# Hash attention and serf feed-forward on one core: a new erf polynomial, log1p and abs re-split over the engines, units taken in pairs

## Chip, cores, metric

One core of a Trainium2 chip, everything in float32. The metric is device time in microseconds (us); each kernel was timed in several executions beside the kernel before on the same chip. Engines: PE is TensorE, DVE is VectorE, ACT is ScalarE, POOL is GpSimd. In a profile row such as `L409 ACT COPY h<-h_ps`, L409 is the line of the kernel's source, and `h<-h_ps` says what is written from what.

## The reference

Attention with a hash mask over 4 x 8 heads of 768 tokens and 64 features, then, on x of 3072 x 512:

```python
h = x @ w_in                                            # 512 -> 2048
sp = np.maximum(h, 0.0) + np.log1p(np.exp(-np.abs(h)))  # softplus
g = h * erf(sp)
return (g @ w_out).astype(np.float32)                   # 2048 -> 512
```

The change touches only this second half.

## The kernel before

The feed-forward works in 48 units; a unit is 256 tokens x 512 features, a tile of 128 x 1024. Per unit: 32 matmul instructions into PSUM (`hidden`), elementwise work on ACT, DVE and POOL, and later 16 matmul instructions with w_out (`project`). Cut to what matters:

```python
def exponential(u):
    nc.scalar.activation(out=a, in_=ps, func=AF.Abs)
    nc.scalar.activation(out=a, in_=a, func=AF.Exp, scale=-1.0)
    nc.scalar.copy(out=h, in_=ps)
    nc.gpsimd.tensor_scalar(out=up, in0=a, scalar1=1.0, scalar2=None, op0=ALU.add)
    nc.vector.scalar_tensor_tensor(out=a, in0=up, scalar=-1.0, in1=a, op0=ALU.add, op1=ALU.subtract)

def softplus(u):
    nc.scalar.activation(out=s, in_=s, func=AF.Ln)                    # s is up
    nc.vector.scalar_tensor_tensor(out=s, in0=h, scalar=0.0, in1=s, op0=ALU.max, op1=ALU.add)
    nc.vector.scalar_tensor_tensor(out=s, in0=s, scalar=S_MAX, in1=a, op0=ALU.min, op1=ALU.subtract)
    nc.scalar.activation(out=z, in_=s, func=AF.Square)
    for k in range(len(ERF_P) - 2, -1, -1):                           # six steps
        nc.vector.scalar_tensor_tensor(out=p, in0=prev, scalar=ERF_P[k] / lead,
                                       in1=z if k else s, op0=ALU.add, op1=ALU.mult)

def gate(u):
    nc.scalar.activation(out=d["p"], in_=d["p"], func=AF.Tanh, scale=ERF_P[-1])
    nc.gpsimd.tensor_tensor(out=d["h"], in0=d["h"], in1=d["p"], op=ALU.mult)

# LAG = NG + 2 = 6 units
for n in range(len(units) + LAG):
    if 0 <= n - 2 < len(units): gate(n - 2)
    if n < len(units): hidden(n); exponential(n)
    if 0 <= n - 1 < len(units): softplus(n - 1)
    if n >= LAG: project(...)
```

One thing about the source matters for all that follows: the framework (`tile.TileContext`) puts the instructions into the engines' queues by a schedule of its own.

## Time and profile before

| | before |
|---|---|
| time, median (range) of 7 runs | 1547.7 us (1547.2 to 1549.3) |
| attention ends, feed-forward's products run on | at 784.3 us |
| period of the units (copies of h, 790.8 to 1496.6, over 47) | 15.0 us |
| PE's own work for a unit | 13.8 us |
| from the last copy of h to the end | 48.8 us |
| activation-table loads | 95 |

The table is read from below upwards: PE needs 13.8 us a unit but is served one only every 15.0 us. The lines behind it are in the prediction.

### The profile page before, as it was taken

What the parts mean: (1) busy time and instruction counts of PE and PEld (TensorE: products, weight loads), DVE (VectorE), ACT (ScalarE), POOL (GpSimd) and SP (SyncE); (2) the same over time, 40 slices, a digit from 0 to 9 for tenths busy, and PEclk for the clock granted to TensorE, in tenths of its full rate; (3) what the DMA queues carried; (4) which work ended last, traced back from release to release, by engine and by line L of the source; (5) the groups of instructions that cost most, each with busy time, mean ns of one, the idle gap of its engine ahead of it and who ended that gap; (6) DMA issues with size and microseconds to landing.
All of it is one profiled execution on the core that took longest, in us unless ns stands there. A gap on an engine that the chain in (4) does not pass through costs nothing. (4 is left out here: it accounts for less than half of the span.)

```text
span 1545.4 us, 14597 instructions
## 1 busy us (share of the span) xinstructions
PE 1441.5 (93%) x5248; PEld 808.8 (52%) x5248; DVE 1187.5 (77%) x1865; ACT 758.9 (49%) x1151; POOL 425.2 (28%) x198
## 2 busy tenths in 40 slices
PE   7999999999999999999997898999999999999977
PEld 3444444444445444445575565656565556656543
DVE  6788878888786666666637799888887887878783
ACT  2344444444444444444555554565555555555551
POOL 3333223332220000000013433433433333333340
PEclk9999999999999999999998999999999999999989
DMA  5222222222211011010000000000000000000000
GB/s 157 76 63 67 68 77 76 69 67 63 67 36 42 26 36 41 26 37 6 1 1 0 0 9 13 7 8 7 14 7 7 14 7 7 7 14 8 7 8 27
DMA packets 40704, 49.19 MB, mean 32 GB/s; under 512 B 27308, under 2 KB 27320, under 8 KB 40632
## 3 DMA queue, kind: packets, MB, share of 16 engines
q1 hardware_dynamic: 35856, 31.47, 7.0%
q0 software_dynamic: 4608, 16.78, 3.4%
q8 instruction: 42, 0.69, 0.2%
q14 instruction: 30, 0.25, 0.1%
q10 hardware_dynamic: 168, 0.01, 0.0%
HBM read 41.96 MB, written 6.29 MB: 31 GB/s over the span
## 5 line engine op out<-in xcount | busy, mean ns | idle before, releaser
L392 PE MATMUL h_ps<-xT,w_in_sb 128*128 128x256 f32 x1536 | 353.6, 390 | 50.3 <-ACT h L409 50.0
L457 PE MATMUL o_ps<-w_out_sb,h 128*128 128x512 f32 x768 | 343.7, 601 | 20.7 <-POOL h L446 11.5
L392 PEld LDWEIGHTS h_ps<-xT,w_in_sb 128*128 128x128 f32 x1536 | 296.7, 195 | 122.6 <-ACT h L409 77.4
L325 ACT COPY eT<-tr_ps 128x384 f32<-128x384 f32 x384 | 171.0, 481 | 320.8 <-PE tr_ps L318 319.5
L410 POOL TENSOR_SCALAR up<-a 128x1024 f32<-128x1024 f32 x48 | 161.2, 3358 | 604.1 <-ACT a L408 601.7
L275 PE MATMUL sc<-ka,qa 128*128 128x384 f32 x768 | 299.3, 498 | 11.5 <-ACT e L290 10.9
L432 DVE SCALAR_TENSOR_TENSOR p<-p,a 128x1024 f32<-128x1024 f32 x192 | 266.9, 1392 | 5.2
L333 PE MATMUL av<-eT,vt 128*64 128x384 f32 x768 | 262.1, 491 | 0.0
L457 PEld LDWEIGHTS o_ps<-w_out_sb,h 128*128 128x128 f32 x768 | 147.8, 193 | 191.9 <-issue 175.2
L283 DVE TENSOR_REDUCE m<-sc 128x1 f32<-128x768 f32 x192 | 183.1, 954 | 64.1 <-PE sc L275 60.9
L290 ACT ACTIVATE e<-sc,nm 128x768 f32<-128x768 f32 x192 | 173.9, 906 | 90.1 <-DVE nm L285 87.6
L318 PEld LDWEIGHTS tr_ps<-ident,e 128*128 128x128 f32 x1152 | 126.5, 141 | 120.0 <-issue 50.0
L318 PE MATMUL tr_ps<-ident,e 128*128 128x128 f32 x1152 | 177.2, 281 | 6.9 <-DVE e L303 2.4
L333 PEld LDWEIGHTS av<-eT,vt 128*64 128x64 f32 x768 | 100.0, 137 | 154.1 <-issue 146.0
L446 POOL TENSOR_TENSOR h<-h,p 128x1024 f32<-128x1024 f32 x48 | 119.7, 2494 | 194.3 <-issue 160.2
L275 PEld LDWEIGHTS sc<-ka,qa 128*128 128x128 f32 x768 | 126.5, 192 | 69.5 <-ACT e L290 25.6
L303 DVE TENSOR_SCALAR e<-e,r 128x768 f32<-128x768 f32 x192 | 124.3, 647 | 2.8
L445 ACT ACTIVATE p<-p 128x1024 f32<-128x1024 f32 x48 | 50.7, 1056 | 133.7 <-DVE p L432 133.5
L432 DVE SCALAR_TENSOR_TENSOR p<-a 128x1024 f32<-128x1024 f32 x48 | 74.6, 1554 | 43.1 <-ACT a L427 43.1
L340 DVE COPY xT<-av 64x384 f32<-64x384 f32 x64 | 35.3, 551 | 94.2 <-PE av L333 94.1
L411 DVE SCALAR_TENSOR_TENSOR a<-up,a 128x1024 f32<-128x1024 f32 x48 | 71.4, 1488 | 43.0 <-POOL up L410 43.0
L172 POOL TENSOR_SCALAR keep<-keep 128x512 int32<-128x512 int32 x32 | 73.2, 2286 | 92.8 <-DVE nm L285 56.8
(41 smaller groups left out, 1092.7 us busy)
## 6 DMA issues: line engine op xcount, KB each, us to landing
qa<-in_qkT_dram SPq DMA_DIRECT2D x32, 384.0 KB, 3.5
raw<-in_w_in_dram POOLq DMA_DIRECT2D x16, 512.0 KB, 4.3
raw<-in_w_out_dram POOLq DMA_DIRECT2D x16, 512.0 KB, 3.8
ka<-in_qkT_dram SPq DMA_DIRECT2D x32, 192.0 KB, 3.8
vt<-in_v_dram SPq DMA_DIRECT2D x32, 192.0 KB, 2.7
out_dram<-ob SPq DMA_DIRECT2D x24, 256.0 KB, 2.0
powers_f<-in_powers_dram ACTq DMA_DIRECT2D x1, 6.0 KB
proj_sb<-in_proj_dram SPq DMA_DIRECT2D x1, 6.0 KB, 1.7
```

The costliest lines, as they stand in the source:

```text
L275: nc.tensor.matmul(out=sc[:, half, 0:HS], lhsT=d["qa"][:, c * P : (c + 1) * P], rhs=d["ka"][:, half * HS : (half + 1) * HS], start=True, s ...
L283: nc.vector.reduce_max(out=m, in_=sc[:, :, 0:HS], axis=AX.XY)
L290: nc.scalar.activation(out=e[:, :].rearrange("p (h k) -> p h k", h=2), in_=sc[:, :, 0:HS], func=AF.Exp, bias=nm[:, 0:1], scale=scale, accu ...
L303: nc.vector.tensor_scalar(out=e, in0=e, scalar1=r[:, 0:1], scalar2=None, op0=ALU.mult)
L318: nc.tensor.transpose(out=ps[:, j * P : (j + 1) * P], in_=e[:, kc * P : (kc + 1) * P], identity=ident,)
L325: nc.scalar.copy(out=dst, in_=src)
L333: nc.tensor.matmul(out=av[rows, :], lhsT=d["vt"][:, kc, :], rhs=d["eT"][:, kc, :], start=(kc == 0), stop=(kc == NC - 1),)
L392: nc.tensor.matmul(out=ps[:, f, :], lhsT=w_in_sb[:, kc, (g * G + f) * P : (g * G + f + 1) * P], rhs=xT[b][:, kc, t0 : t0 + T], start=(kc = ...
L410: nc.gpsimd.tensor_scalar(out=up, in0=a, scalar1=1.0, scalar2=None, op0=ALU.add)
L432: nc.vector.scalar_tensor_tensor(out=p, in0=prev, scalar=ERF_P[k] / lead, in1=z if k else s, op0=ALU.add, op1=ALU.mult,)
L446: nc.gpsimd.tensor_tensor(out=d["h"], in0=d["h"], in1=d["p"], op=ALU.mult)
L457: nc.tensor.matmul(out=ps, lhsT=st[t * NG + f // G]["h"][:, f % G, tt * P : (tt + 1) * P], rhs=w_out_sb[:, f, :], start=(f == 0), stop=(f ...
```

## The change

Its intent: take work off DVE (a polynomial as a product of three sums of squares, three DVE steps instead of six, at the price of three Squares on ACT), read h_ps only once, clear h's sign bit on DVE instead of Abs on ACT, take ln(1 + e) with the bias inside the activation, and take the units in pairs so that Exps and Tanhs of a pair share one activation-table load and Lns another. The core of the diff, comments and renamings cut:

```diff
+    def take(u):
+        nc.scalar.copy(out=h, in_=d.pop("ps"))
+        nc.vector.tensor_scalar(out=e(I32), in0=h(I32), scalar1=0x7FFFFFFF, op0=ALU.bitwise_and)
     def exponential(u):
-        Abs, Exp, Copy on ACT; 1 + e on POOL; (up - 1) - a on DVE
+        nc.scalar.activation(out=e, in_=e, func=AF.Exp, scale=-1.0)
+        nc.vector.tensor_scalar(out=w, in0=e, scalar1=1.0, scalar2=-1.0, op0=ALU.add, op1=ALU.add)
     def softplus(u):
-        nc.scalar.activation(out=s, in_=s, func=AF.Ln)
+        nc.scalar.activation(out=s, in_=e, func=AF.Ln, bias=1.0)
+        nc.gpsimd.tensor_tensor(out=w, in0=e, in1=w, op=ALU.subtract)
         (two scalar_tensor_tensor on DVE, as before)
+    def polynomial(u):
+        nc.scalar.activation(out=z, in_=p, func=AF.Square)
+        for j, (_, r) in enumerate(ERF_Q):                 # three pairs (c, r)
+            nc.scalar.activation(out=q, in_=z, func=AF.Square, bias=cq[:, j : j + 1])
+            nc.vector.scalar_tensor_tensor(out=q, in0=q, scalar=r, in1=p, op0=ALU.add, op1=ALU.mult)
+            p = q
-    for n in range(len(units) + LAG): ...
+    NB = NU // 2
+    for k in range(NB + 2):
+        for j in range(2):
+            if k < NB: hidden(2 * k + j)
+            if k >= 2: project((k - 2) // 2, (k - 2) % 2, j)
+            if k < NB: take(2 * k + j)
+            if 1 <= k <= NB: polynomial(2 * (k - 1) + j)
+        for j in range(2): exponential(2 * k + j)          # if k < NB
+        for j in range(2): gate(2 * (k - 1) + j)           # if 1 <= k <= NB
+        for j in range(2): softplus(2 * k + j)             # if k < NB
```

More of the change, by code (lines that the diff above doesn't have):

```diff
@@ L44 @@
 S_MAX = 4.0
-ERF_P = (
-    1.128379274299137,
-    0.10276905585663672,
-    -0.00019183094772544265,
-    -0.0006197845329948793,
-    8.76372797726047e-05,
-    -5.668467798142407e-06,
-    1.418517747371711e-07,
+ERF_LEAD = 1.418517747371711e-07
+ERF_Q = (
+    (6.2794604751645355, 19.35174303303216),
+    (-5.316226701641483, 239.37499811839012),
+    (-20.943483610527835, 66.98472325796595),
 )
@@ L375 @@
                 turn(t // NC, t % NC, done.pop(t))
-    hp = ctx.enter_context(tc.tile_pool(name="hp", bufs=10))
-    work = ctx.enter_context(tc.tile_pool(name="work", bufs=3))
+    cq = const.tile([P, len(ERF_Q)], F32, name="cq")
+    for j, (c, _) in enumerate(ERF_Q):
+        nc.vector.memset(cq[:, j : j + 1], c)
+    hp = ctx.enter_context(tc.tile_pool(name="hp", bufs=8))
+    ew = ctx.enter_context(tc.tile_pool(name="ew", bufs=2))
+    sp = ctx.enter_context(tc.tile_pool(name="sp", bufs=4))
+    work = ctx.enter_context(tc.tile_pool(name="work", bufs=2))
     outp = ctx.enter_context(tc.tile_pool(name="outp", bufs=2))
     ps_h = ctx.enter_context(tc.tile_pool(name="ps_h", bufs=2, space=PSUM))
-    ps_o = ctx.enter_context(tc.tile_pool(name="ps_o", bufs=2, space=PSUM))
-    units = [(t, g) for t in range(NT // T) for g in range(NG)]
+    ps_o = ctx.enter_context(tc.tile_pool(name="ps_o", bufs=4, space=PSUM))
+    NU = (NT // T) * NG
     st = {}
     def hidden(u):
-        t, g = units[u]
+        t, g = divmod(u, NG)
         b, t0 = t // TPB, (t % TPB) * T
@@ L399, in hidden @@
         st[u] = dict(ps=ps)
+    def take(u):
+        d = st[u]
+        h = d["h"] = hp.tile([P, G, T], F32, name="h", tag="h")
+        e = d["e"] = ew.tile([P, G, T], F32, name="e", tag="e")
+        nc.scalar.copy(out=h, in_=d.pop("ps"))
+        nc.vector.tensor_scalar(
+            out=e[:, :, :].bitcast(I32),
+            in0=h[:, :, :].bitcast(I32),
+            scalar1=0x7FFFFFFF,
+            scalar2=None,
+            op0=ALU.bitwise_and,
+        )
     def exponential(u):
         d = st[u]
-        ps = d["ps"]
-        h = hp.tile([P, G, T], F32, name="h", tag="h")
-        a = work.tile([P, G, T], F32, name="a", tag="a")
-        up = work.tile([P, G, T], F32, name="up", tag="up")
-        nc.scalar.activation(out=a, in_=ps, func=AF.Abs)
-        nc.scalar.activation(out=a, in_=a, func=AF.Exp, scale=-1.0)
-        nc.scalar.copy(out=h, in_=ps)
-        nc.gpsimd.tensor_scalar(out=up, in0=a, scalar1=1.0, scalar2=None, op0=ALU.add)
-        nc.vector.scalar_tensor_tensor(
-            out=a, in0=up, scalar=-1.0, in1=a, op0=ALU.add, op1=ALU.subtract
+        e = d["e"]
+        w = d["w"] = ew.tile([P, G, T], F32, name="w", tag="w")
+        nc.scalar.activation(out=e, in_=e, func=AF.Exp, scale=-1.0)
+        nc.vector.tensor_scalar(
+            out=w, in0=e, scalar1=1.0, scalar2=-1.0, op0=ALU.add, op1=ALU.add
         )
-        d.update(h=h, a=a, up=up)
     def softplus(u):
         d = st[u]
-        h, a, s = d["h"], d["a"], d["up"]
-        nc.scalar.activation(out=s, in_=s, func=AF.Ln)
+        h, e, w = d["h"], d.pop("e"), d.pop("w")
+        s = d["s"] = sp.tile([P, G, T], F32, name="s", tag="s")
+        nc.scalar.activation(out=s, in_=e, func=AF.Ln, bias=1.0)
+        nc.gpsimd.tensor_tensor(out=w, in0=e, in1=w, op=ALU.subtract)
         nc.vector.scalar_tensor_tensor(
@@ L423, in softplus @@
         nc.vector.scalar_tensor_tensor(
-            out=s, in0=s, scalar=S_MAX, in1=a, op0=ALU.min, op1=ALU.subtract
+            out=s, in0=s, scalar=S_MAX, in1=w, op0=ALU.min, op1=ALU.add
         )
-        z = a
-        nc.scalar.activation(out=z, in_=s, func=AF.Square)
-        p = work.tile([P, G, T], F32, name="p", tag="p")
-        lead = ERF_P[-1]
-        prev = z
-        for k in range(len(ERF_P) - 2, -1, -1):
-            nc.vector.scalar_tensor_tensor(
-                out=p,
-                in0=prev,
-                scalar=ERF_P[k] / lead,
-                in1=z if k else s,
-                op0=ALU.add,
-                op1=ALU.mult,
+    def polynomial(u):
+        d = st[u]
+        p = d.pop("s")
+        z = work.tile([P, G, T], F32, name="z", tag="z")
+        nc.scalar.activation(out=z, in_=p, func=AF.Square)
+        for j, (_, r) in enumerate(ERF_Q):
+            last = j == len(ERF_Q) - 1
+            q = z if last else work.tile([P, G, T], F32, name=f"q{j}", tag=f"q{j}")
+            nc.scalar.activation(out=q, in_=z, func=AF.Square, bias=cq[:, j : j + 1])
+            nc.vector.scalar_tensor_tensor(
+                out=q, in0=q, scalar=r, in1=p, op0=ALU.add, op1=ALU.mult
             )
-            prev = p
+            p = q
         d["p"] = p
@@ L444, in gate, with project @@
         d = st[u]
-        nc.scalar.activation(out=d["p"], in_=d["p"], func=AF.Tanh, scale=ERF_P[-1])
-        nc.gpsimd.tensor_tensor(out=d["h"], in0=d["h"], in1=d["p"], op=ALU.mult)
+        p = d.pop("p")
+        nc.scalar.activation(out=p, in_=p, func=AF.Tanh, scale=ERF_LEAD)
+        nc.gpsimd.tensor_tensor(out=d["h"], in0=d["h"], in1=p, op=ALU.mult)
     o_live = {}
-    def project(t, part):
-        tt, half = divmod(part, 2)
+    def project(t, half, tt):
         if half == 0:
-            o_live[t] = ps_o.tile([P, DM], F32, name="o_ps", tag="o")
-        ps = o_live[t]
+            o_live[tt] = ps_o.tile([P, DM], F32, name="o_ps", tag="o")
+        ps = o_live[tt]
         for f in range(half * NF // 2, (half + 1) * NF // 2):
@@ L468, in project @@
             nc.sync.dma_start(out=out[r0 : r0 + P, :], in_=ob)
-            if tt == 1:
-                for g in range(NG):
-                    st.pop(t * NG + g)
-    LAG = NG + 2
-    for n in range(len(units) + LAG):
-        if 0 <= n - 2 < len(units):
-            gate(n - 2)
-        if n < len(units):
-            hidden(n)
-            exponential(n)
-        if 0 <= n - 1 < len(units):
-            softplus(n - 1)
-        o = n - LAG
-        if o >= 0:
-            project(o // NG, o % NG)
+        if tt == 1:
+            for g in range(half * NG // 2, (half + 1) * NG // 2):
+                st.pop(t * NG + g)
+    NB = NU // 2
+    for k in range(NB + 2):
+        for j in range(2):
+            if k < NB:
+                hidden(2 * k + j)
+            if k >= 2:
+                project((k - 2) // 2, (k - 2) % 2, j)
+            if k < NB:
+                take(2 * k + j)
+            if 1 <= k <= NB:
+                polynomial(2 * (k - 1) + j)
+        for j in range(2):
+            if k < NB:
+                exponential(2 * k + j)
+        for j in range(2):
+            if 1 <= k <= NB:
+                gate(2 * (k - 1) + j)
+        for j in range(2):
+            if k < NB:
+                softplus(2 * k + j)
 _OUT = ((3072, 512), "float32")
```

## The prediction

> **What bounds the kernel now.** I read the page first (busy shares, slices), then the windows of the feed-forward, the instructions of the tile h_ps, the groups by shape, and the timeline of a few units and of the end.
>
> ```profile
> PE 1441.5 (93%) x5248; PEld 808.8 (52%) x5248; DVE 1187.5 (77%) x1865; ACT 758.9 (49%) x1151; POOL 425.2 (28%) x198
> PEclk9999999999999999999998999999999999999989
> 900.00:1500.00 600.00, 555.34 (x1863) 356.78 (x1861) 496.30 (x378) 335.20 (x314) 232.01 (x80) 0.98 0.02 9
> 784.29 30.92 PE L392 MATMUL h_ps<-xT,w_in_sb 128*128 128x256 f32 x142
> L409 ACT COPY h<-h_ps x48: 997/1003/1007, 790.8 to 1496.6; 128x1024 f32<-128x1024 f32 x48
> ```
>
> The attention is over at 784.3 us, where the 30.92 us run of w_in products starts; eight of the first unit's 32 had already been slipped in before. The diff leaves the attention alone, so 784.3 us stay. The feed-forward has 48 units of 256 tokens x 512 features. PE's floor for one: 31 starts in (7.07 - 0.38) us give 0.216 us a w_in product, and 47 starts in (20.76 - 0.59) us give 0.429 us a w_out product (rows below); 32 x 0.216 + 16 x 0.429 = 13.8 us. The real period is that of the copies: (1496.6 - 790.8) / 47 = 15.0 us. So PE loses 1.2 us a unit in the steady part, though it looks 93% busy.
>
> ```profile
> 1464.32 1.06 ACT L427 ACTIVATE a<-up 128x1024 f32<-128x1024 f32 x1 [2.55 <-DVE up L423]
> 1465.28 1.00 ACT L407 ACTIVATE a<-h_ps 128x1024 f32<-128x1024 f32 x1
> 1466.18 1.00 ACT L409 COPY h<-h_ps 128x1024 f32<-128x1024 f32 x1
> 1466.66 5.72 DVE L432 SCALAR_TENSOR_TENSOR p<-p,a 128x1024 f32<-128x1024 f32 x4
> 1467.24 8.86 PE L392 MATMUL h_ps<-xT,w_in_sb 128*128 128x256 f32 x32 [2.26 <-ACT h L409]
> ...
> 1475.94 20.76 PE L457 MATMUL o_ps<-w_out_sb,h 128*128 128x512 f32 x48
> ...
> 1522.26 19.13 PE L457 MATMUL o_ps<-w_out_sb,h 128*128 128x512 f32 x40 [4.21 <-POOL h L446]
> ```
>
> PE waits 2.26 us for h_ps, which is read twice (Abs, Copy). These reads stand on ACT behind a Square that waited 2.55 us for DVE. DVE is the slow side of this ring: 496.3 us busy in 600 us is 12.4 us a unit, and the round trips (to ACT for Ln and Square, to POOL for 1+e) add the rest of 15.0. **The bound is the ring of DVE and its waits, not PE.** At the end, unit 47's chain runs alone, and 40 w_out products come after it in 19.13 us.
>
> **What the Trainium skill says.** (1) "ScalarE: Activation LUTs", Table sets: exp and tanh share a set, so calls should be batched by set; a load is about 1283 ns. The trace agrees: 95 loads of 1283 ns, alternating between Ln on one side and Exp or Tanh on the other, none before Square or Copy. (2) "VectorE: DVE Perf Modes", The perf-mode tier table: float32 tensor_scalar has a two-elements mode, two-tensor forms don't. The trace agrees: 0.62 us for 768 elements with one tensor, 1.24 us for 1024 with two. (3) "SBUF — State Buffer", SBUF: two separate sides: DVE with two SBUF inputs and GpSimd lock a shared port pair against each other. The trace agrees for the tensor_tensor on POOL: it starts at 825.40 and takes 2.34, and the DVE instruction beside it takes 3.35 instead of 1.22, ending 1.1 us after it (second and third row here).
>
> ```profile
> L303 DVE TENSOR_SCALAR e<-e,r x15: 598/620/621, 703.3 to 753.9; 128x768 f32<-128x768 f32 x15
> 825.40 2.34 POOL L446 TENSOR_TENSOR h<-h,p 128x1024 f32<-128x1024 f32 x1
> 825.47 3.35 DVE L411 SCALAR_TENSOR_TENSOR a<-up,a 128x1024 f32<-128x1024 f32 x1 [2.66 <-POOL up L410]
> 1118.22 7.07 PE L392 MATMUL h_ps<-xT,w_in_sb 128*128 128x256 f32 x32
> ```
>
> (4) "TensorE: Matmul & The Clock Gate", Part 1: after an idle window of about 3.4 us the array runs at half clock until it has been busy as long. The trace agrees in kind: the 40 products after a 4.21 us gap took 19.13 us, where 40 x 0.429 is 17.2, so 2 us lost.
>
> **The change, part by part, for one unit.** *DVE* loses the five or so two-tensor steps of the polynomial and the (u-1)-e step: ten two-tensor instructions per unit become five (two in softplus, three in the polynomial), 5 x 1.24 = 6.2 us; it gains two single-tensor ones (clearing the sign bit, and (e+1)-1). Scaling 0.62 us at 768 I estimate 0.7 us each, 1.4; output copies 0.68/2 = 0.3. Sum 7.9 instead of 12.4 us. *ACT* drops Abs and adds three Squares: Copy, Exp, Ln, Tanh, four Squares, 8 x 1.05 = 8.4 us; table loads fall from 2 a unit to 2 a pair, 1.3 us. Sum 9.7 of 13.8, still no bound. *POOL* exchanges 1+e (3.3 us) for e-w (a tensor_tensor, 2.34): 2 x 2.34 = 4.7 us. *PE*'s work is the same. h_ps is now free after one 1.0 us copy that stands on ACT without DVE before it. The lag from hidden to project shrinks from six units to two pairs.
>
> **Does the new ring fit under PE?** One turn without PE, for a pair: Tanh 1.1, two gates and two subtractions on POOL 9.4, the last two softplus steps 2.5 to 3.5, four Squares 4.2, table load 1.3, two Exps 2.1: about 21.6 us. PE needs 2 x 13.8 = 27.6 us. So it fits, and PE should run nearly gapless. The port pair carries, for a pair, ten two-tensor steps 12.4, four POOL instructions 9.4 and four single-tensor 2.8: 24.6 of 27.6 us. Full, but under.
>
> One tight place is left. Every second pair, the output copy stands on DVE ahead of the second unit's sign-clearing and polynomial, and waits for PE's project. Counted from the end of that unit's hidden: project 6.9, copy 0.7, sign 0.7, Exp 1.1, Tanh 1.1, gate 2.3 plus up to 1.3 waiting for the port: 12.8 to 14.1, with half a microsecond for hand-overs, and the second gate 2.4 later. PE comes for these at 13.8 (project, next hidden) and 3.4 later. I put in a mean stall of 0.8 us in each of the 12 such pairs: 9.6 us.
>
> **The sum.** Start 784.3. PE's remaining work: 48 x 13.77 less eight products of 0.216 = 659.3. *Head:* pair 0 must pass the whole chain before the first project. Counting from hidden 0's end at 789.9: hidden 1 to 796.8, Exps 799.9, load and Lns 803.2, s(0) 804.7, pair 1's copies wait for hidden 3 at 810.4, Squares of unit 1 to 815.6, load and Exps 819, Tanh 820, gate 822.5; PE has run out at 817.2: 5.3 idle, 2 for the clock. *Stalls* 9.6. *Tail:* after the last hidden PE has five half-blocks left (34 us), but pair 22's gates come 6.2 us too late, as no hidden fills that gap any more, and the last pair's softplus, Squares, Tanh and gate another 9.6: 15.8 idle and 4 for the clock. Last copy and store 4.0, as now (1541.4 to 1545.4). Together 784.3 + 659.3 + 7.3 + 9.6 + 19.8 + 4.0 = 1484.3 us of span; the timed median is 2.0 above the span today, so **1486 us**, 61 us or 4.0% less.
>
> **Rivals.** (a) *The port pair becomes the bound.* For it: 89% of it is booked, and DVE and POOL will be woken together by the same Tanh and Ln. Against it: POOL works in one clump of some 10 us a pair, and the polynomials lie outside it. If each pair lost 1.5 us, 24 x 1.5 = 36 instead of 9.6: 1512 us. (b) *PE was the bound all along, and only head and tail change.* For it: 93% busy and "PE o_ps" at the end of the chain. Against it: the 15.0 us period against 13.8. It would give some 1535 to 1545 us. (c) *The table batching is the gain.* Two loads saved per pair are 2.6 us of ACT, but ACT is 56% busy (335.2 of 600); by itself that moves little. (d) *No stalls at all* and a shorter tail: 784.3 + 659.3 + 7 + 12 + 6 = 1469 us.
>
> **Range and chances.** Low is (d), high lies near (a), with an error of a few us in head and tail: 1469 to 1507. The 2% line is 1516 us; only (a) beyond its estimate, or (b), reach it. Faster 0.92, within 2% 0.07, slower 0.01.
>
> **What would show each step.** Copies from h_ps 27 to 28.5 us a pair in place of 30; PE's granted clock 0.99 or 1.00 between 900 and 1400 us; DVE near 60%, ACT near 70% of the steady part; 48 or so table loads; waits of PE for h_ps gone, what remains being waits for POOL's h in odd pairs; the mean of the two-tensor steps above 1.24 us only where POOL works; first w_out product near 822 us. I am wrong if the period stays near 30 us a pair with DVE idle under 10% (port), if PE waits for h_ps still (the copy is held on ACT), or if attention's end moves.

## The result, and the profile after

| | before | after |
|---|---|---|
| time, median of 4 runs each | 1547.6 us | 1537.4 us (1537.1 to 1537.7) |
| ratio | | 0.9935 (0.9921 to 0.9949) |
| first to last copy of h, over 47 | 15.02 us | 15.15 us |
| the last 32 of these periods alone | 15.20 us | 15.67 us |
| last copy of h to the end of the span | 48.8 us | 34.5 us |
| activation-table loads | 95 | 97 |

Ratios in this document are the mean time of one kernel's fast runs over that of the other's of the same rounds, so not quite the ratio of the medians that are quoted. The change gained 10 us, not 61. The first row of the changed kernel's page:

```profile
PE 1435.7 (94%) x5248; PEld 805.3 (52%) x5248; DVE 1080.8 (70%) x1772; ACT 874.9 (57%) x1249; POOL 379.0 (25%) x198
```

Its table loads, from the groups by shape (count, busy time, mean ns of one, idle time before them):

```profile
L433 ACT ACT_TABLE_LOAD x48 | 61.6, 1283 | 0.8
L460 ACT ACT_TABLE_LOAD x38 | 48.8, 1283 | 0.7
L423 ACT ACT_TABLE_LOAD x10 | 12.8, 1283 | 4.3 <-DVE e L411 4.2
```

The copies of h, from the instructions of its tile h_ps (their ns, then the times of the first and the last):

```profile
L410 ACT COPY h<-h_ps x48: 988/992/1012, 788.7 to 1500.8; 128x1024 f32<-128x1024 f32 x48
```

DVE did lose work (70% busy instead of 77%), and ACT got it (57% instead of 49%), as predicted. But there are still two table loads a unit, and the period is no shorter: (1500.8 - 788.7) / 47 = 15.15 us. The whole gain is at the ends: the first copy is 2.1 us earlier and the end comes 34.5 instead of 48.8 us after the last copy, 14.3 us less, while the 47 periods took 6.3 us more. That is 10.1 us, the difference of the spans (1545.4 and 1535.3). The mean over 47 hides the filling at the start: there the changed kernel's first four periods are 7 to 10 us each. Over the last 32 it is slower than the kernel before: (1500.82 - 999.28) / 32 = 15.67 us, against (1496.57 - 1010.07) / 32 = 15.20.

Here is one unit of the steady part, from the changed kernel's timeline (start, duration, engine, line, what; in brackets the idle time before it and what ended it):

```profile
1106.14 1.06 ACT L446 ACTIVATE z<-s 128x1024 f32<-128x1024 f32 x1 [4.54 <-DVE s L438]
1107.23 2.19 ACT L450 ACTIVATE q<-z,cq 128x1024 f32<-128x1024 f32 x2
...
1109.45 1.15 ACT L450 ACTIVATE z<-z,cq 128x1024 f32<-128x1024 f32 x1
...
1110.50 0.99 ACT L410 COPY h<-h_ps 128x1024 f32<-128x1024 f32 x1
...
1111.51 1.28 ACT L460 ACT_TABLE_LOAD   x1
1111.55 7.17 PE L397 MATMUL h_ps<-xT,w_in_sb 128*128 128x256 f32 x32 [1.54 <-ACT h L410]
...
1112.81 1.06 ACT L460 ACTIVATE z<-z 128x1024 f32<-128x1024 f32 x1
1113.77 1.04 ACT L423 ACTIVATE e<-e 128x1024 f32<-128x1024 f32 x1
...
1114.83 1.28 ACT L433 ACT_TABLE_LOAD   x1
1114.84 2.00 DVE L424 TENSOR_SCALAR w<-e 128x1024 f32<-128x1024 f32 x1 [1.94 <-ACT e L423]
...
1116.12 1.06 ACT L433 ACTIVATE s<-e 128x1024 f32<-128x1024 f32 x1
...
1116.92 2.35 POOL L434 TENSOR_TENSOR w<-e,w 128x1024 f32<-128x1024 f32 x1 [0.63 <-DVE w L424]
1117.37 2.99 DVE L435 SCALAR_TENSOR_TENSOR s<-h,s 128x1024 f32<-128x1024 f32 x1
...
1121.72 1.06 ACT L446 ACTIVATE z<-s 128x1024 f32<-128x1024 f32 x1 [4.54 <-DVE s L438]
```

**This is not the order of the source.** The source has two Exps, two Tanhs, two Lns in a row, and the Squares of a pair only in the next turn. In this turn ACT ran: Copy, load, Tanh (of the unit before), Exp, load, Ln, and then the four Squares *of the same unit*. In that order the Squares wait for the softplus that has only just begun (4.54 us of idle ACT), and the next Copy, which frees h_ps for PE, stands behind the Squares. The turn takes 1121.72 - 1106.14 = 15.58 us, and PE waits 1.54 us of it. Two waits for the port pair of DVE and POOL (the prediction's point 3) lie in this ring: DVE's (e + 1) - 1 takes 2.00 us instead of 0.69 beside POOL's gate and so holds up POOL's subtraction, and the first softplus step takes 2.99 us instead of 1.2 beside that subtraction.

In the steady part the turns repeat in eights: four of 15.6 us like this one, then 14.4, 17.4, 17.0 and 14.2, in which the order differs again (Exp carries the load, or Tanh stands ahead of the copy), but the Squares always follow their own unit's softplus. Their mean is the 15.67 us of the table. Why the framework chose these orders no run shows.

Theory A: the lost gain is the order. Rivals: the port pair of DVE and POOL is the bound whatever the order (B); PE's own work is 15 us (C).

### The profile page after: what moved, and what is told of

Read it like the earlier page. It is cut to its first block, busy times and chain, and to the rows that moved or that the text cites. A ratio compares the mean times of both kernels' runs of the same rounds, so it can differ in the third digit from the quotient of the medians.

```text
span 1535.3 us, 14770 instructions
## 1 busy us (share of the span) xinstructions
PE 1435.7 (94%) x5248; PEld 805.3 (52%) x5248; DVE 1080.8 (70%) x1772; ACT 874.9 (57%) x1249; POOL 379.0 (25%) x198
## 4 chain that ended last, share of the span: by engine, by line
PE 37%; DVE 27%; ACT 26%; issue 7%; POOL 2%; DMA 1%; POOLq 0%; SPq 0%; DVEq 0%; ACTq 0%
PE av L332 13%; PE sc L274 11%; DVE s L435 7%; PE tr_ps L317 7%; ACT q L450 5%; DVE s L438 3%; ACT e L423 3%; ACT z L446 3%; DVE m L282 3%; ACT L433 3%; DVE q L451 2%; ACT h L410 2%; PE bits_ps L225 2%; ACT L460 2%; ACT s L433 2%
## 5 line engine op out<-in xcount | busy, mean ns | idle before, releaser
L397 PE MATMUL h_ps<-xT,w_in_sb 128*128 128x256 f32 x1536 | 349.0, 386 | 44.1 <-ACT h L410 43.9
L397 PEld LDWEIGHTS h_ps<-xT,w_in_sb 128*128 128x128 f32 x1536 | 293.6, 193 | 115.9 <-ACT h L410 69.9
L434 POOL TENSOR_TENSOR w<-e,w 128x1024 f32<-128x1024 f32 x48 | 114.7, 2389 | 487.1 <-DVE w L424 487.1
L461 POOL TENSOR_TENSOR h<-h,z 128x1024 f32<-128x1024 f32 x48 | 119.8, 2497 | 357.2 <-ACT z L460 357.2
L435 DVE SCALAR_TENSOR_TENSOR s<-h,s 128x1024 f32<-128x1024 f32 x48 | 118.5, 2468 | 37.2 <-ACT s L433 37.2
L446 ACT ACTIVATE z<-s 128x1024 f32<-128x1024 f32 x48 | 50.7, 1056 | 157.6 <-DVE s L438 157.6
L451 DVE SCALAR_TENSOR_TENSOR q<-q,s 128x1024 f32<-128x1024 f32 x48 | 62.8, 1308 | 91.3 <-ACT q L450 91.3
L424 DVE TENSOR_SCALAR w<-e 128x1024 f32<-128x1024 f32 x48 | 66.7, 1389 | 73.4 <-ACT e L423 73.4
L450 ACT ACTIVATE q<-z,cq 128x1024 f32<-128x1024 f32 x96 | 105.1, 1140 | 1.4
```

The costliest lines, as they stand in the source:

```text
L397: nc.tensor.matmul(out=ps[:, f, :], lhsT=w_in_sb[:, kc, (g * G + f) * P : (g * G + f + 1) * P], rhs=xT[b][:, kc, t0 : t0 + T], start=(kc = ...
L450: nc.scalar.activation(out=q, in_=z, func=AF.Square, bias=cq[:, j : j + 1])
L461: nc.gpsimd.tensor_tensor(out=d["h"], in0=d["h"], in1=p, op=ALU.mult)
```

## The experiments

All outputs are right. To hold an order, the framework has a call that queues an instruction behind the one traced before it on the same engine; it is meant as an order of issue and adds no work. "Held" below means that each feed-forward instruction of the engines named went through it. (With all four engines held the trace has as many PE, DVE and POOL instructions as the changed kernel's, and on ACT only the table loads are fewer: 1201 instead of 1249.)

### Held in the written order

```diff
+    keep = tc.keep_in_program_order
-        nc.scalar.copy(out=h, in_=d.pop("ps"))
+        keep(nc.scalar.copy(out=h, in_=d.pop("ps")))
   (and so for every nc.tensor, nc.vector, nc.scalar and nc.gpsimd call of the feed-forward)
```

> The changed kernel with one thing added: in the feed-forward every PE, DVE, ACT and POOL instruction is held behind the one written before it for its engine. Theory A (the order of the instructions: the kernel that ran was not in the written order, each unit's Copy, Tanh, Exp, Ln, Squares came one unit at a time, so two table loads a unit and every Square directly behind the softplus of its own unit): 48 or so table loads instead of 95, copies from h_ps 27.6 to 28.5 us a pair, and the time of the prediction, 1475 to 1500 us. Theory B (the port pair of DVE and POOL is the bound, whatever the order): the period stays near 30 us a pair, 1525 us or more. Theory C (PE's own work is the bound, 15 us a unit): within 10 us of 1537.

Measured: 1485.75 us (1485.4 to 1486.9), ratio 0.9598 (0.9583 to 0.9612). Table loads 49 in all. From the timeline of this run:

```profile
1126.46 2.00 ACT L424 ACTIVATE e<-e 128x1024 f32<-128x1024 f32 x2
1128.37 1.99 ACT L461 ACTIVATE z<-z 128x1024 f32<-128x1024 f32 x2
1130.38 1.28 ACT L434 ACT_TABLE_LOAD   x1
```

Two Exps, two Tanhs, one load, as written. The row of its windows for 900 to 1400 us (after the length of the stretch come the busy times, PE's first; the third number from the end is the granted clock):

```profile
900.00:1400.00 500.00, 497.15 (x1727) 327.13 (x1726) 357.59 (x270) 343.07 (x324) 186.54 (x72) 1.00 0.03 10
```

And PE's rows of the end, from the timeline:

```profile
1438.21 16.77 PE L472 MATMUL o_ps<-w_out_sb,h 128*128 128x512 f32 x32 [6.04 <-POOL h L462]
1463.12 16.27 PE L472 MATMUL o_ps<-w_out_sb,h 128*128 128x512 f32 x32 [8.13 <-POOL h L462]
```

Between 900 and 1400 us PE is busy 497.15 of 500 at a granted clock of 1.00. What is left are gaps at the start and the end: in the two rows of the end PE waits 6.04 and 8.13 us, and 32 products take 16.8 and 16.3 us instead of 13.9 (31 x 0.429 + 0.59). B and C are out: the same instructions, with the same port and the same PE work, run 52 us faster in another order. The port waits are still there (the two softplus steps take 2.04 and 2.25 us on average), but they no longer decide when PE is served.

### Only ACT held; ACT and POOL held

```diff
   keep(...) around nc.scalar calls only                  (first run)
   keep(...) around nc.scalar and nc.gpsimd calls only    (second run)
```

> The changed kernel with only the ACT instructions of the feed-forward held in the written order. Theory A, if ACT's order alone matters: within 8 us of the run in which all four engines are held. If DVE's or PE's place in the order matters as well (an output copy standing in front of a sign clearing): 10 us or more away from it, on either side.

Measured: 1612.1 us, ratio 1.0413 (1.0397 to 1.0430): 126 us above the run with all four held, the largest surprise. Holding one engine moved the others' order too. From its timeline:

```profile
1126.98 2.36 POOL L435 TENSOR_TENSOR w<-e,w 128x1024 f32<-128x1024 f32 x1 [0.70 <-DVE w L425]
...
1129.30 6.61 POOL L462 TENSOR_TENSOR h<-h,z 128x1024 f32<-128x1024 f32 x2
...
1132.68 9.82 PE L472 MATMUL o_ps<-w_out_sb,h 128*128 128x512 f32 x16 [3.63 <-POOL h L462]
```

POOL takes the pair's subtractions (L435) ahead of the gates (L462), which is not the source's order either, and PE waits 3.63 us for the gated h, long enough for its clock to fall: 9.82 us instead of 7.03 for 16 products.

> The changed kernel with the ACT and the POOL instructions of the feed-forward held in the written order, DVE and PE as they come. In the run with ACT alone held, POOL did both subtractions of a pair ahead of the two gates, and PE waited for the gated h (3.6 us in each pair of a period of 34 us). If that swap is the cause of the 1612 us: 1480 to 1500 us now. If DVE's order (both first softplus steps ahead of both second ones, the output copy in between) is the cause: 1580 us or more.

Measured: 1473.6 us, ratio 0.9520 (0.9506 to 0.9535), a little below the range given. In its trace DVE still does both first softplus steps of a pair ahead of both second ones, as in the run before. So POOL's swap, two instructions, was the cause of the 1612 us, and DVE's order was not. It is 12 us faster than all four held: PE, left free, filled the start with products of the next units (its gap there is 3.29 us instead of 6.05), and its two gaps at the end are 5.28 and 6.63 us instead of 6.04 and 8.13.

### Squares held directly behind their own unit's softplus

```diff
-        take(n); polynomial(n - 2); exponential(n); gate(n - 2); softplus(n)
+        take(n); gate(n - 1); exponential(n); softplus(n); polynomial(n)
```

This is against the run in single units further down (project still four units behind); it holds the order in which ACT was seen in the turn above. Not only the Squares move: the gate stands one unit behind instead of two, and project and its output copy stand later in the turn.

> The changed arithmetic held in the order in which ACT was seen to run it: a unit's Copy, the Tanh of the unit before, Exp, Ln, and its four Squares directly behind. It differs from the run in held single units (1474) only in where the polynomial stands (the same unit instead of two behind), where the gate stands and in the output copy's place. If that place is the cause of the lost gain: a ring over ACT and DVE of about 15.6 us a unit, ACT waiting some 4.5 us a unit for softplus, 1530 to 1575 us. If the cause is something else in the order that was not held: below 1500 us.

Measured: 1560.0 us, ratio 1.0083 (1.0067 to 1.0099). From its timeline:

```profile
1113.44 1.06 ACT L447 ACTIVATE z<-s 128x1024 f32<-128x1024 f32 x1 [4.54 <-DVE s L439]
...
1118.85 7.17 PE L398 MATMUL h_ps<-xT,w_in_sb 128*128 128x256 f32 x32 [1.54 <-ACT h L411]
```

The changed kernel's ring is there to the hundredth: ACT waits 4.54, PE waits 1.54, copies (1522.9 - 793.2) / 47 = 15.53 us apart. In the steady part (15.6 us a unit) that is no slower than the changed kernel with its mixture of orders (15.67 us). That the whole run is 23 us longer comes from the start: here the periods are 15.6 us from the second on and the fifth copy comes at 852.9 us, in the changed kernel at 824.3. So this run gives back the ring of the steady part, not the whole time of the changed kernel.

### The subtraction moved from POOL to DVE

```diff
-        nc.gpsimd.tensor_tensor(out=w, in0=e, in1=w, op=ALU.subtract)
+        nc.vector.tensor_tensor(out=w, in0=e, in1=w, op=ALU.subtract)
```

> The changed kernel with the subtraction e - w moved from POOL to DVE, order otherwise left as it comes; it was seen beforehand that ACT still goes Copy, Tanh, Exp, Ln, four Squares a unit. Theory B' (on the ring as it runs, waiting for the port pair is part of the 15.58 us: the first softplus step takes 3.15 instead of 1.2 us): the ring shrinks by about 1.1 us to 14.5 us a unit, ACT's wait for softplus falls from 4.5 to about 3.4 us, 1490 to 1510 us. If the port wait is hidden behind something else: within 10 us of 1537.

Measured: 1506.9 us, ratio 0.9733 (0.9719 to 0.9748), in the range expected. The copies are (1468.4 - 788.9) / 47 = 14.46 us apart, the last 32 of these periods 14.94 us (15.67 in the changed kernel). From its timeline:

```profile
1117.74 1.22 DVE L435 SCALAR_TENSOR_TENSOR s<-h,s 128x1024 f32<-128x1024 f32 x1
...
1120.31 1.06 ACT L446 ACTIVATE z<-s 128x1024 f32<-128x1024 f32 x1 [4.07 <-DVE s L438]
```

The first softplus step takes 1.22 us again. ACT's wait fell only to 4.07 us in the turns where the output copy came between (15.1 us a turn), and to 3.47, as expected, in those without it (14.5 us). So the move is worth 30 us in this ring, which has no slack. How much of that is the port wait and how much the subtraction's own shorter time (1.23 us on DVE, 2.35 on POOL) the run does not separate. In the held order the same move costs a little:

> Both: all four engines in the written order, and e - w on DVE. If PE is the bound in the written order and the port pair costs only the stalls of every second pair that were put at 0.8 us each: 0 to 12 us below the run in written order alone. If DVE, with 1.2 us more a unit, is now in the way: above it.

Measured: 1492.2 us, ratio 0.9641 (0.9625 to 0.9657), 6 us above the held order with the subtraction on POOL. PE's waits for the gated h rose from 23.4 to 30.6 us, which is about the difference. DVE was not busier for it (350.6 us of the 500 between 900 and 1400, against 357.6), so its amount of work is not the reason; which step of the chain came later was not traced.

### The distance from hidden to project, and single units

```diff
-            if k >= 2: project((k - 2) // 2, (k - 2) % 2, j)
+            if k >= 3: project((k - 3) // 2, (k - 3) % 2, j)     # NB + 3 turns; all four held
```

> All four engines in the written order, and project three pairs behind hidden instead of two (eight buffers of h are enough for it). Theory: what is left above PE's work in the run in written order is one gap at the start (6.05 us, and 2.5 us of the first project at the lower clock) and two at the end (6.04 and 8.13 us, and some 5 us of clock), because PE has nothing else to do while a pair passes through the chain. With one more pair in between PE has 27 us more of hidden at the start, and 14 us more of project at the end: the gap at the start goes, those at the end shrink to one of 0 to 4 us: 1455 to 1468 us. If the gaps come from something else: within 8 us of the run in written order (1486).

Measured: **1455.0 us** (1454.3 to 1455.6), ratio 0.9403 (0.9388 to 0.9419), the fastest. The row of its windows:

```profile
900.00:1400.00 500.00, 500.00 (x1746) 331.56 (x1746) 363.26 (x277) 351.14 (x332) 194.94 (x76) 1.00 0.03 10
```

The end of its timeline:

```profile
1398.90 34.50 PE L472 MATMUL o_ps<-w_out_sb,h 128*128 128x512 f32 x80
1434.80 14.00 PE L472 MATMUL o_ps<-w_out_sb,h 128*128 128x512 f32 x32 [1.41 <-POOL h L462]
```

PE is busy all of the steady part; the 14 us of gaps at the end are one of 1.41 us, and the last 32 products take 14.0 us, at full clock. The feed-forward of this kernel is bound by PE.

```diff
   # all four held, loop over single units n, same functions
+    hidden(n); project(half-block n - 4); take(n); polynomial(n - 2)
+    exponential(n); gate(n - 2); softplus(n)
```

> The changed arithmetic, all four engines held, but in single units with the same distances (polynomial two units behind, project four), so without batching by activation table: about 95 table loads again, ACT some 11 of 13.8 us a unit. If the batching itself is worth something: 15 us or more above the run in written order by pairs (1486). If, as the prediction's rival (c) says, it moves little as long as ACT is not the bound: within 10 us of it, or below it, as the tight place behind the output copy goes.

Measured: 1473.8 us, ratio 0.9524 (0.9509 to 0.9538). 12 us *faster* than by pairs at the same distance, with 97 table loads instead of 49. The batching by table is worth nothing here, as ACT is not the bound; what this order has in common with the one by pairs is that the Squares stand well behind their softplus (here two units); moved next to it, 1560 us came out.

```diff
-            k, j = divmod(n - 4, 2)      # project four units behind
+            k, j = divmod(n - 6, 2)      # six
```

> Single units in held order, with project six units behind hidden instead of four. If the gaps at start and end are what is left there as well: 1450 to 1458 us, the same as by pairs with the longer distance, as PE is then the bound in both and the number of table loads is of no account.

Measured: 1457.0 us (1454.9 to 1459.9), ratio 0.9412 (0.9396 to 0.9428). Pairs or single units, with the distance long enough it is the same.

### How much is owed to the arithmetic

```diff
   the kernel before, all four engines held in its own source order
```

> The kernel before (its arithmetic, its loop) with all four engines of the feed-forward held in the written order. Theory A says that it is the order and not the holding that counts, and the written order of this one is bad: Abs, Exp, 1+e on POOL, (u-1)-e, softplus, Square and the whole polynomial of DVE follow one another with Tanh ahead of Abs on ACT, some 19 us a unit by the durations of the trace: 1680 to 1780 us. If holding an order helps by itself: below 1545 us.

Measured once, so of unknown state: 1715.4 us. Holding is no gain by itself; the source order of the kernel before is a bad one, and the free schedule had improved it.

```diff
   the kernel before, free order, with the new polynomial (three Squares, three DVE steps)
```

> The kernel before with one part of the change alone: the polynomial as three squares on ACT and three two-tensor steps on DVE; the rest and the order as they come. It was seen beforehand that ACT's order is still Abs, Copy, Exp, Tanh and Ln, four Squares directly behind the softplus of the same unit. Theory A: DVE loses 3.7 us a unit, but the ring over ACT takes over (three Squares of 1.1 us more between Ln and the next Abs), so little comes of it: 1500 to 1560 us. If DVE's work was the bound as such: 1460 to 1490 us.

Measured: 1592.7 us, ratio 1.0290 (1.0274 to 1.0305), slower than the kernel before and beyond the range given for theory A: PE waited up to 4.5 us for the copy of h. The part that takes 3.7 us a unit off DVE made the kernel 45 us slower. Its three more Squares stand on the same ACT as that copy, which is the likely cause; the free schedule may have moved other instructions too, and no run separates the two.

```diff
   the kernel before, all held: Abs, Copy (n); polynomial (n - 2); Exp, 1+e (n); gate (n - 3); (u-1)-e, Ln, softplus (n - 1)
   (and four buffers instead of three for its work tiles)
```

> The arithmetic of the kernel before (polynomial of degree six on DVE, Abs on ACT, 1+e on POOL), but with the stages of a unit one unit apart (softplus one behind the exponential, polynomial two, gate three) and all four engines held in that order. Is the new arithmetic needed at all? If only the order mattered: PE becomes the bound here too, 1455 to 1485 us. If the old DVE work is too much: nine two-tensor steps of 1.24 and the output copy are 11.5 us a unit, and POOL blocks DVE for 2.3 us (gate) and some 1.1 us (1+e) a unit, together 14.9 us against PE's 13.8: 1505 to 1550 us.

Measured: 1605.3 us, ratio 1.0368 (1.0351 to 1.0385), above both expectations. One of its four executions took 4287.7 us, with PE's products some three times as long in the records; no other run showed this, and it is left unexplained. (In the last session one execution of the kernel before took 1825.8 us at a clock of 0.752; it counts as slow, like this one, and is in no ratio.) As the profile fell there, the kernel was run again:

> The same kernel as the one before with its stages spread (1605 us, whose profile fell in an execution of 4288 us that none of the timed ones shows again). Only for its profile: a period of about 16.4 us a unit, DVE idle at most 1.5 us of it, and two-tensor steps above 1.24 us beside POOL's work, if DVE and the port pair bound it; if it is an in-order wait on ACT: DVE idle 3 us or more a unit.

Measured: 1603.9 us. The row of its windows:

```profile
900.00:1500.00 600.00, 538.83 (x1790) 348.21 (x1789) 520.13 (x352) 314.61 (x297) 206.32 (x74) 0.94 0.02 8
```

A row of its timeline:

```profile
1114.02 7.83 DVE L441 SCALAR_TENSOR_TENSOR p<-p,a 128x1024 f32<-128x1024 f32 x4
```

The third busy time is DVE's: 520 of 600 us, and four of its steps take 7.83 us beside POOL, instead of the 5.00 us that four such steps take in the run below. The copies are 16.2 us apart (1126.14 - 1109.93), of which DVE is idle 80 / 600, 2.2 us. So neither reading alone fits: it is DVE with its port waits, and waits for Ln and Square on top (1.1 and 0.8 us a unit).

```diff
   single units, distance six (1457 us), with the old polynomial: one Square, six DVE steps
```

> Single units in held order with the longer distance (1457), with one part undone: the polynomial of degree six on DVE as before (six two-tensor steps, one Square). What is the new polynomial worth when PE is the bound? DVE then has eight two-tensor steps, two single-tensor ones and the output copy, 11.6 us a unit, and POOL's two instructions lock it out for up to 4.7 us: 14 to 16.3 us a unit against PE's 13.8: 1480 to 1580 us. If the port waits fall into gaps of DVE: 1455 to 1470 us, and the new polynomial is worth nothing once the order is good.

Measured: 1611.8 us, ratio 1.0417 (1.0398 to 1.0435), above the range. From its timeline:

```profile
1117.33 3.41 DVE L435 SCALAR_TENSOR_TENSOR s<-h,s 128x1024 f32<-128x1024 f32 x1 [2.89 <-ACT s L433]
...
1130.74 1.06 ACT L465 ACTIVATE p<-p 128x1024 f32<-128x1024 f32 x1 [5.04 <-DVE p L451]
```

In this order Tanh waits 5.04 us for the long polynomial, Ln stands behind Tanh, and DVE waits 2.89 us for Ln: a ring of 1130.74 - 1113.87 = 16.87 us. So in this order the new polynomial is worth 155 us, and the old arithmetic (all of it in two runs, its polynomial alone in this one) was slower than the kernel before in each of the three held orders tried. That no order at all would bring it down to PE's bound is not shown.

## Why the prediction was wrong

**The step that failed** is one that the text took for granted: that each engine runs its instructions in the order in which the source has them. It stands in two of its sentences. "h_ps is now free after one 1.0 us copy that stands on ACT without DVE before it": in the kernel that ran, the copy stands behind four Squares (in some turns behind a Tanh too), and these behind up to 4.54 us of waiting for DVE, so that a unit took 15.67 us in the steady part and not 13.8. And "table loads fall from 2 a unit to 2 a pair": 97 loads were counted. From there the ring of 21.6 us a pair, the stalls and the ends were worked out for a program that was never run.

**Shown, not argued:** the kernel with the written order and nothing else added took 1485.75 us where 1486 was predicted, and an order with the Squares directly behind their softplus gives the slow ring of the steady part back to the hundredth (4.54 and 1.54 us).

**The terms, for the held run.** Predicted and measured: start of the run of products 784.3 and 783.7; gap at the start 5.3 and 6.05, its clock loss 2 and 2.5; gaps at the end 15.8 and 14.2, their clock loss 4 and some 5; last copy and store 4.0 and 4.2. The stalls behind the output copy, put at 9.6 in all, were 3.2 us (PE waited 23.4 us for h in total, of which 20.2 are those gaps). PE's work was about 5 us longer than 659.3: none of its products slipped into the attention, which is 1.7 of them (8 x 0.216); the rest was not traced. The two nearly cancel, so the close agreement of the sums is partly luck; the mechanism is not. DVE was put at 7.9 us a unit; in the held run it is busy 357.59 of 500 us, 10 us a unit (72%, not near 60%), with the waits for the port. That was too low, but there it was not the bound.

**The rivals.** (a), the port pair, has a true core: its waits are in the ring that ran (2.00 and 2.99 us, above), and moving the subtraction to DVE gave 30 us. But it is not the bound: in the held order POOL keeps both instructions, and PE is the bound. (b) named the right size for the wrong reason: the gain lies in head and tail, but PE's work was not 15 us. (c) was rightly set aside: the number of table loads moves nothing while ACT has room (1457.0 us with 97, 1455.0 with 49).

**The signs it missed.** The text's own list of what would make it wrong has "PE waits for h_ps still (the copy is held on ACT)", which is what came, but without a probability. And the trace of the kernel before showed that order is not the source's: its source has Abs, Exp, Copy; the rows in the prediction have Abs, then Copy, directly behind each other. The row was quoted, and its meaning was not drawn. The text also counts ten two-tensor steps before; there were nine, and the polynomial lost three, not five or so. And its point (4), on the clock, agrees less well than it says: in its own rows 32 products after a gap of only 2.26 us took 8.86 us instead of 7.07. The kernel before has eleven gaps of 2.1 to 2.3 us, and slow products followed four of them; in the run with ACT and POOL held the products after a gap of 3.29 us took 7.13 us, nearly full speed. The length of a gap alone does not tell.

## What to carry to other kernels

Before a pipeline is worked out from the source, compare the source's order with the engine's order in the trace, unit by unit; if a framework schedules, an intended software pipeline is a wish until it is held. Hold all engines of a stage or check each of them, as holding ACT alone made this kernel 126 us slower than holding all. When PE is the bound, what is left lies at the two ends: a longer distance between producer and consumer stages, for no more buffers here, gave another 31 us, while halving the table loads gave none.

## What the Trainium skill lacked or had wrong

- "ScalarE: Activation LUTs", What ACT_TABLE_LOAD costs: it gives about 2.66 us for every switch, a load of 1283 ns and a drain of about 1380 ns. The load is right; the drain is not seen in the changed kernel's turn: the Copy of 0.99 us starts at 1110.50, the load at 1111.51, the next function at 1112.81, so a switch costs 1.3 us here.
- The same page, Table sets: "Batch activation calls by set". Right for ACT's time, but it doesn't say that it pays nothing where ACT has room: with 97 loads the kernel was as fast as with 49 (1457.0 and 1455.0 us).
- "SBUF — State Buffer", SBUF: two separate sides: DVE with two SBUF inputs and GpSimd block each other for the whole instruction. Seen for POOL's two-input form (2.99 us instead of 1.22 beside it). Not so beside POOL's one-input form: in the kernel before (the prediction's row of 5.72 us) POOL's instruction ran 3.40 us from 1469.64, and the DVE step that started at 1470.44 ended before it did, after 1.94 us.
- No page says how to check in a trace whether a scheduling framework kept the source's order on an engine, or what it can cost if it did not. Here it made the difference between 1537 and 1486 us.
